# A pruned matmul whose first tiles use packed weights: eight tiles with the upper K half packed in place of seven tiles with both halves

## The chip, the cores and the metric

The kernel runs on one core of one Trainium2 chip. The time is that of the device, in microseconds (us). Most executions agree within 0.3%. All runs compared here are in the fast state, with a granted TensorE clock of 1.0 (0.998 at the least) unless a number says otherwise.

A profile is taken of one execution per kernel. Its span, from the first to the last instruction, is about 2 us shorter than the time. PE is TensorE (matmuls), PEld its weight loads, DVE VectorE, ACT ScalarE, POOL GpSimd, SP the engine that issues most DMAs. HBM is the memory outside the core (DRAM in the kernel's words), SBUF the memory inside it that the engines work from, PSUM the banks that TensorE writes its sums to. K is the dimension that a matmul sums over.

## The reference, cut to what matters

```python
B, S, D = 16, 512, 1024                      # bf16
wg   = w.reshape(256, 4, 1024)               # groups of 4 along K
mag  = abs(wg)
thr  = second largest of each group of 4
wp   = (wg * (mag >= thr)).reshape(1024, 1024)
out  = x @ wp + b                            # x: 8192 rows of 1024
```

In tiles of 128 rows that is 64 row tiles. Each needs 16 matmuls of 512 columns: 8 slices of K times 2 halves of the output columns.

Of the kernel before, what the change touches and what calls it, by code (L numbers as in the profile page):

```python
# [10 lines left out]
def kernel(  # L11
# [28 lines left out]
    NPK = 7  # L40
    batches = []
    t0 = NPK
    while t0 < NT:
        nb = min((5, 4)[len(batches)] if len(batches) < 2 else 8, NT - t0)
        batches.append((t0, nb))
        t0 += nb

    const = ctx.enter_context(tc.tile_pool(name="const", bufs=1))
    dram = ctx.enter_context(tc.tile_pool(name="dram", bufs=1, space=bass.MemoryType.DRAM))
# [7 lines left out]

    def rows(t):
        if t < NPK:
            return of[:NPK * P].rearrange("(p t) f -> p t f", t=NPK)[:, t, :]  # L60
        return of[t * P:(t + 1) * P, :]
# [21 lines left out]

    zeros = const.tile([P, P], bf16)
    dve(nc.vector.memset(zeros[:], 0.0))  # L85
    spark = const.tile([P, P], bf16)

# [4 lines left out]
    xv = xf[:NPK * P].rearrange("(p t) k -> p t k", t=NPK)  # L92
# [9 lines left out]
    def load_x(ta, tb, g, eng="sp"):  # L102
        xs = const.tile([P, tb - ta, HK], bf16, name=f"x_{ta}_{g}")
        issue(eng, xs[:], xv[:, ta:tb, g * HK:(g + 1) * HK])
        for t in range(ta, tb):
            x_sb[(t, g)] = xs[:, t - ta, :]


    load_w(0, 0, 256)
    load_x(6, 7, 0, "act")  # L110
    act(nc.scalar.activation(spark[:, :1], zeros[:, :1], Act.Abs))
    load_x(4, 6, 0)
    load_x(2, 4, 0)
    load_w(0, 256, 512)
    load_x(6, 7, 1)
    load_x(1, 2, 0)
    load_w(1, 256, 512)
    load_x(2, 4, 1)
    load_w(1, 0, 256)
    load_x(4, 6, 1)  # L120
    load_w(0, 512, 1024)
    load_x(0, 2, 1)
    load_x(0, 1, 0)
    load_w(1, 512, 1024)
    sp(nc.sync.dma_start(bias_sb[:], b.partition_broadcast(P)))


    pieces = [(0, 0, 256), (0, 256, 512), (1, 0, 256), (1, 256, 512), (0, 512, 1024), (1, 512, 1024)]
# [12 lines left out]
    scratch = dram.tile([D, Dout], bf16, name="wp_scratch")  # L141
    scr_pk = scratch.rearrange("(g q m) f -> q g m f", g=G, m=4)
    scr_nat = scratch.rearrange("(kt p) f -> p kt f", p=P)
# [40 lines left out]
    def save(g, c0, c1, eng="sp"):  # L184
        issue(eng, scr_pk[:, g, :, c0:c1], wp[:, g, :, c0:c1])

    def reload(h):
        fs = slice(h * FH, (h + 1) * FH)
        sp(nc.sync.dma_start(wp_nat[:, :, fs], scr_nat[:, :, fs]))

    xpk = {}

    def transpose(t, g):


        xg = x_sb[(t, g)].rearrange("p (q m) -> p m q", m=4)
        tp = psum_t.tile([P, 4, P], bf16, name="tp")
        for m in range(4):
            pe(nc.tensor.transpose(tp[:, m, :], xg[:, m, :], ident[:]))  # L199
        xpk[(t, g)] = tp  # L200

    def copy_xt(t, g):
        xt = xtp.tile([P, 4, P], bf16, name=f"xt{g}")
        act(nc.scalar.copy(xt[:].bitcast(fp32), xpk[(t, g)][:].bitcast(fp32)))  # L204
        xpk[(t, g)] = [xt[:, m, :] for m in range(4)]

    ps_open = {}

    part = {"": slice(0, 4), "x": slice(0, 2), "y": slice(2, 4)}
    opened = []  # L210
    left = {}

    def mm_piece(t, i, ms):
        g, c0, c1 = pieces[i]
        h = c0 // FH
        new = (t, h) not in ps_open
        if new:
            ps_open[(t, h)] = psum_o.tile([P, FH], fp32, name="ps")
            opened.append((t, h))
            left[(t, h)] = sum(4 for pc in pieces if pc[1] // FH == h)  # L220
        ps = ps_open[(t, h)]
        for m in range(ms.start, ms.stop):
            left[(t, h)] -= 1
            pe(nc.tensor.matmul(ps[:, c0 - h * FH:c1 - h * FH], lhsT=xpk[(t, g)][m],  # L224
                                rhs=wp[:, g, m, c0:c1],
                                start=(new and m == ms.start), stop=(left[(t, h)] == 0),
                                skip_group_check=True))
# [3 lines left out]
    def stage(t):  # L231
        st = stg.tile([P, FH], fp32, name="st")
        act(nc.scalar.copy(st[:], ps_open.pop((t, 0))[:]))  # L233
        staged[t] = st

    def finish(t):
        o = outp.tile([P, Dout], bf16, name="o")
        dve(nc.vector.tensor_tensor(o[:, FH:], ps_open.pop((t, 1))[:], bias_sb[:, FH:], op=Alu.add))  # L238
        dve(nc.vector.tensor_tensor(o[:, :FH], staged.pop(t)[:], bias_sb[:, :FH], op=Alu.add))  # L239
        issue("act", rows(t), o[:])  # L240

    xnat = {}

    def load_batch(bi):
        if bi >= len(batches):
            return
        tb, nb = batches[bi]
        xb = xtb.tile([P, KT, 8 * P], bf16, name="xb")
        sp(nc.sync.dma_start_transpose(out=xb[:, :, :nb * P], in_=xf[tb * P:(tb + nb) * P, :]))
        for j in range(nb):  # L250
            xnat[tb + j] = xb[:, :, j * P:(j + 1) * P]



# [3 lines left out]
            "T6a F5 T5a T4a F6 T3a T2a F7 M5.0y M4.0y M6.0y M2.0y M5.0x M3.0x T6b T1a M6.0x M3.0y "  # L258
            "M4.0x M2.0x M1.0y M1.0x T3b T2b M6.1 M4.1 M3.1 T4b M1.1 M5.1 T5b M2.1 M6.3 M3.3 M4.3 "
            "T1b T0b M5.3 M2.3 M1.3 M3.2 M6.2 M5.2 T0a M4.2 M2.2 M1.2 M0.0y M0.1 M0.2 M0.3 M0.0x "  # L260
            "M2.4 M3.4 M1.4 M0.4 M5.4 M4.4 M5.5 M2.5 M1.5 M4.5 M6.4 M0.5 M6.5 M3.5"
        ),
        "dve": (
            "abs0 hi0 lo0 t10 t20 thr0 mask0y mask0x mult0y abs1 mult0x hi1 lo1 t11 t21 thr1 mask1 "
            "mult1 lo3 hi3 t23 t13 thr3 mask3 mult3 lo2 hi2 t22 t12 thr2 mask2 mult2 lo4 hi4 t24 "
            "t14 thr4 mask4 mult4 hi5 lo5 t25 t15 thr5 mask5 mult5"
        ),
        "act": (
            "C6a C5a C4a C2a C3a C6b C1a abs3 C3b abs2 C2b C4b C5b abs4 C1b abs5 C0a S5 C0b S1 S4 "
            "S6 S2 S0 S3 W5 W4"  # L270
# [4 lines left out]

    halves = {0: ('x', 'y')}
# [10 lines left out]
    def needs(eng, tok):  # L287
# [7 lines left out]
        if base[0] == "M":  # L295
            t, i = base[1:].split(".")
            key = (int(t), pieces[int(i)][1] // FH)
            slot = []
            if key not in opened and len(opened) >= 6:
                pt, ph = opened[len(opened) - 6]  # L300
                slot = [f"S{pt}"] if ph == 0 else []
            return [f"C{t}{'ab'[pieces[int(i)][0]]}", f"mult{i}{k}"] + slot
        if tok[0] == "S":
            return [f"M{tok[1:]}.{n}" for i, pc in enumerate(pieces) if pc[1] < FH for n in all_of(str(i), i)]
        if tok[0] == "W":
            return all_of("mult" + tok[1:], int(tok[1:]))
# [5 lines left out]
    def emit(eng, tok):  # L312
        base, k = split_tok(tok)
        if tok[0] == "T":
            transpose(int(tok[1]), "ab".index(tok[2]))
# [3 lines left out]
        elif tok[0] == "C":  # L319
            copy_xt(int(tok[1]), "ab".index(tok[2]))  # L320
        elif tok[0] == "M":
            mm_piece(*map(int, base[1:].split(".")), part[k])
        elif tok[0] == "S":
            stage(int(tok[1:]))
        elif tok[0] == "W":
            save(*pieces[int(tok[1:])], eng="act")
        else:
            i = int(base[-1])
            if i not in p:
                p[i] = Piece(i)  # L330
            if eng == "act":
                p[i].abs_act()
            else:
                p[i].do(base[:-1], part[k])
# [14 lines left out]
    save(0, 0, 256)  # L349
    save(0, 256, 512)  # L350
    save(1, 0, 256)
    save(1, 256, 512)
    load_batch(0)
    reload(0)
    reload(1)
    load_batch(1)
    load_batch(2)
    for t in (2, 0, 3, 1, 6, 5, 4):
        finish(t)


    def nat_group(xt, ps, c0, c1):
        for kt in range(KT):
            pe(nc.tensor.matmul(ps, lhsT=xt[:, kt, :], rhs=wp_nat[:, kt, c0:c1],  # L364
                                start=(kt == 0), stop=(kt == KT - 1)))

    def evac(o, ps, c0, c1):
        dve(nc.vector.tensor_tensor(o[:, c0:c1], ps, bias_sb[:, c0:c1], op=Alu.add))  # L368
# [3 lines left out]

    for bi, (tb, nb) in enumerate(batches):
        load_batch(bi + 3)
        if bi == 0:
            outs = [outp.tile([P, Dout], bf16, name="o") for _ in range(nb)]
            for h in range(2):
                for j in range(nb):
                    ps = psum_o.tile([P, FH], fp32, name="ps")
                    nat_group(xnat[tb + j], ps[:], h * FH, (h + 1) * FH)  # L380
                    evac(outs[j], ps[:], h * FH, (h + 1) * FH)
                    if h == 1:
                        store("act", tb + j, outs[j])
            continue
        for j in range(nb):
# [3 lines left out]
            if t == NT - 1:  # L389
                for n, (c0, c1) in enumerate(((0, FH), (FH, FH + CW), (FH + CW, Dout - P), (Dout - P, Dout))):  # L390
                    ps = psum_o.tile([P, FH], fp32, name="ps")
                    nat_group(xt, ps[:, :c1 - c0], c0, c1)
                    evac(o, ps[:, :c1 - c0], c0, c1)
                    store("act" if n % 2 else "sp", t, o, c0, c1)
            else:
                pss = [psum_o.tile([P, FH], fp32, name="ps") for _ in range(2)]
                for kt in range(KT):
                    for h in range(2):
                        pe(nc.tensor.matmul(pss[h][:], lhsT=xt[:, kt, :],  # L399
                                            rhs=wp_nat[:, kt, h * FH:(h + 1) * FH],  # L400
                                            start=(kt == 0), stop=(kt == KT - 1)))
                for h in range(2):
                    evac(o, pss[h][:], h * FH, (h + 1) * FH)
                    if t >= NT - 6:
                        store("act", t, o, h * FH, (h + 1) * FH)
                if t < NT - 6:
# [31 lines left out]
```

## The kernel before: the parts that the change and the argument touch

The pruning compares the four rows of a group. The kernel loads w "packed", with partition q holding rows 4q to 4q+3 side by side, so that the comparison stays inside a partition. A matmul with packed weights needs x permuted in the same way. The first tiles get that from TensorE transposes. All later tiles use "natural" weights (partition = row of K) and take x from transposing DMA loads.

The name `g` is the K half (0 upper, 1 lower) and `h` the half of the output columns. Pruned packed weights reach the natural layout through a scratch tensor in DRAM:

```python
NPK = 7                                           # tiles with packed weights, both K halves
xv = xf[:NPK*P].rearrange("(p t) k -> p t k", t=NPK)     # rows 14 KB apart
pieces = [(0,0,256),(0,256,512),(1,0,256),(1,256,512),(0,512,1024),(1,512,1024)]
... # order lists: T = transpose, C = copy, M tile.piece = products, S = stage PSUM, F = filler
run({eng: order[eng].split() for eng in order})
save(0, 0, 256); save(0, 256, 512); save(1, 0, 256); save(1, 256, 512)   # pruned -> DRAM, SP queue
load_batch(0)                                     # transposing DMA load, 5 tiles
reload(0); reload(1)                              # DRAM -> natural weights, 1 MB each
load_batch(1); load_batch(2)
for t in (2, 0, 3, 1, 6, 5, 4): finish(t)         # bias added, row stored
... # then 57 tiles with natural weights, 16 matmuls each
```

PSUM has six banks for products. The fillers `F` are matmuls on zeros that keep TensorE busy at the start.

## Time and profile before

| | before |
|---|---|
| time, median of 4 runs | 235.28 us (235.03 to 235.44) |
| span of the profiled run | 232.9 us |
| first product with packed weights | 6.86 us |
| first product with natural weights | 33.19 us |
| TensorE idle from the first product to the last | 0.0 us |
| HBM read / written | 6.29 / 18.87 MB |

"Idle" is my own sum over the trace. It takes the starts of consecutive matmuls, and counts what they lie apart beyond 0.216 us (512 columns), 0.109 (256) or 0.056 (128). A distance of exactly two steps is not counted: it is a matmul whose record is missing. The trace of before lacks 20 (1164 matmuls to 1184 weight loads).

These are lines of the profile page of before: busy times, the chain of waits by engine, the costliest groups (line, engine, operation, operands, count, then busy us and mean ns, then idle), and one DMA issue with its us to landing.

```profile
PE 228.2 (98%) x1164; PEld 112.6 (48%) x1184; DVE 104.2 (45%) x177; ACT 15.2 (7%) x27; POOL 0.7 (0%) x6
...
PE 98%; issue 1%; DVE 0%
...
L399 PE MATMUL ps<-wp_nat,xb 128*128 128x512 bf16 x800 | 175.4, 379 | 0.8
...
L199 PE MATMUL tp<-ident,x 128*128 128x128 bf16 x56 | 4.8, 221 | 0.0
...
wp_nat<-wp_scratch SPq DMA_DIRECT2D x2, 1024.0 KB, 6.3
```

TensorE is the limit: 98% of the chain that ended last. A mean of 379 ns for a 512-column matmul is not its cost, because matmuls overlap. The cost is the distance between starts, 0.216 us.

The chain of waits of before, in order of time (start us, length us, what), shows the same without any other engine in it:

```profile
6.89 1.44 PE ps L224 x12
...
21.54 10.74 PE ps L224 x49
...
32.33 1.03 PE ps L224 x4
33.35 9.71 PE ps L364 x45
```

L224 are packed products and L364 the first natural ones. TensorE goes from one to the other at 33.2 us without a gap. Each of the two reloads brings one half of the output columns. The first had landed at 29.5 us. The second landed at 38.9 us; its columns are wanted only after the first half of five tiles, 40 matmuls of 0.216 us later, at about 41.8.

### The profile page before, as it was taken

The numbers are of one execution on the slowest core, as the hardware profiler recorded it, in microseconds if no ns is written. First come the engines' busy times: TensorE is split into PE (matmuls) and PEld (weight loads), VectorE is DVE, ScalarE is ACT, GpSimd is POOL, SyncE is SP. The second block draws the span as 40 slices with busy tenths as digits, with TensorE's granted clock in tenths as the row PEclk, the third lists the DMA queues.
The fourth block names the chain that finished last, engine by engine and source line by source line (L and its number), as shares of the span: only waits on it lengthen the run. The fifth ranks groups of instructions, "written<-read, shape, count | busy, mean of one in ns | idle before, by whom it ended". The sixth has DMA issues, their size and how long they took to land.

```text
span 232.9 us, 2851 instructions
## 1 busy us (share of the span) xinstructions
PE 228.2 (98%) x1164; PEld 112.6 (48%) x1184; DVE 104.2 (45%) x177; ACT 15.2 (7%) x27; POOL 0.7 (0%) x6
## 2 busy tenths in 40 slices
PE   8999999999999999999999999999999999999995
PEld 5997444444444444444444444444444444444443
DVE  3999559533244244244234334334324424423434
ACT  4678000000000000000000000000000000000000
POOL 1000000000000000000000000000000000000000
PEclk9999999999999999999999999999999999999999
DMA  6999969999999952992239821696221221122122
GB/s 191 327 303 242 322 217 223 297 267 256 243 332 261 259 160 77 225 266 98 90 81 274 231 92 45 156 254 178 90 90 54 83 93 64 71 90 91 48 89 90
DMA packets 79500, 40.29 MB, mean 173 GB/s; under 512 B 60416, under 2 KB 71936, under 8 KB 79488
## 3 DMA queue, kind: packets, MB, share of 16 engines
q1 hardware_dynamic: 68208, 22.32, 43.3%
q10 hardware_dynamic: 11280, 17.80, 23.1%
q8 instruction: 9, 0.15, 0.3%
q14 instruction: 3, 0.02, 0.0%
HBM read 6.29 MB, written 18.87 MB: 108 GB/s over the span
## 4 chain that ended last, share of the span: by engine, by line
PE 98%; issue 1%; DVE 0%
PE ps L399 75%; PE ps L224 10%; PE ps L364 9%; PE ps L136 2%; PE tp L199 1%; DVE o L368 0%; DVE zeros L85 0%
## 5 line engine op out<-in xcount | busy, mean ns | idle before, releaser
L399 PE MATMUL ps<-wp_nat,xb 128*128 128x512 bf16 x800 | 175.4, 379 | 0.8
L368 DVE TENSOR_TENSOR o<-ps,bias_sb 128x512 bf16<-128x512 f32 (+1 forms) x116 | 74.0, 677 | 117.2 <-PE ps L399 106.5
L399 PEld LDWEIGHTS <-xb 128*128 128x128 bf16 x816 | 79.8, 98 | 96.4
L224 PE MATMUL ps<-wp,xt 128*128 128x256 bf16 (+1 forms) x166 | 25.3, 307 | 0.1
L364 PE MATMUL ps<-wp_nat,xb 128*128 128x512 bf16 (+2 forms) x110 | 21.0, 348 | 0.1
L224 PEld LDWEIGHTS <-xt 128*128 128x128 bf16 x168 | 16.2, 98 | 7.6
L364 PEld LDWEIGHTS <-xb 128*128 128x128 bf16 x112 | 10.4, 98 | 10.7
L238 DVE TENSOR_TENSOR o<-ps,bias_sb 128x512 bf16<-128x512 f32 x7 | 4.8, 686 | 4.9 <-PE ps L224 4.9
L136 PE MATMUL ps<-zeros 128*128 128x128 bf16 (+1 forms) x32 | 5.1, 320 | 1.0 <-DVE zeros L85 1.0
L159 ACT ACTIVATE mag<-w_sb 128x1024 bf16<-128x1024 bf16 (+1 forms) x4 | 6.0, 1489 | 0.8 <-DMA w_sb<-in_w_dram 0.8
L156 DVE TENSOR_TENSOR wp<-w_sb,mag 128x1024 bf16<-128x1024 bf16 (+2 forms) x7 | 5.4, 765 | 0.2
L156 DVE TENSOR_TENSOR mag<-mag,hi 128x1024 bf16<-128x1024 bf16 (+2 forms) x7 | 5.3, 767 | 0.2
L204 ACT COPY xt<-tp 128x256 f32<-128x256 f32 x14 | 5.0, 372 | 5.2 <-PE tp L199 5.1
L199 PE MATMUL tp<-ident,x 128*128 128x128 bf16 x56 | 4.8, 221 | 0.0
L239 DVE TENSOR_TENSOR o<-st,bias_sb 128x512 bf16<-128x512 f32 x7 | 4.8, 681 | 0.0
L199 PEld LDWEIGHTS <-x 128*128 128x128 bf16 x56 | 4.1, 115 | 0.1
L136 PEld LDWEIGHTS <-zeros 128*128 128x128 bf16 x32 | 2.8, 118 | 2.6 <-issue 1.7
L233 ACT COPY st<-ps 128x512 f32<-128x512 f32 x7 | 3.6, 609 | 0.1
L156 DVE TENSOR_TENSOR hi<-mag 128x512 bf16<-128x512 bf16 (+1 forms) x6 | 3.0, 508 | 0.0
L156 DVE TENSOR_TENSOR lo<-mag 128x512 bf16<-128x512 bf16 (+1 forms) x6 | 3.0, 506 | 0.0
L156 DVE TENSOR_TENSOR hi<-hi,lo 128x256 bf16<-128x256 bf16 (+1 forms) x6 | 2.0, 336 | 0.2
L166 DVE TENSOR_SCALAR mag<-w_sb 128x1024 uint16<-128x1024 uint16 x2 | 0.8, 424 | 2.8 <-DMA w_sb<-in_w_dram 2.8
(11 smaller groups left out, 6.4 us busy)
## 6 DMA issues: line engine op xcount, KB each, us to landing
out_dram<-o ACTq DMA_DIRECT2D x58, 256.0 KB, 3.9
wp_nat<-wp_scratch SPq DMA_DIRECT2D x2, 1024.0 KB, 6.3
x<-in_x_dram SPq DMA_DIRECT2D x5, 256.0 KB, 4.7
out_dram<-o ACTq DMA_DIRECT2D x10, 128.0 KB, 1.7
w_sb<-in_w_dram SPq DMA_DIRECT2D x4, 256.0 KB, 4.2
w_sb<-in_w_dram SPq DMA_DIRECT2D x2, 512.0 KB, 7.0
wp_scratch<-wp SPq DMA_DIRECT2D x4, 256.0 KB, 5.7
wp_scratch<-wp ACTq DMA_DIRECT2D x2, 512.0 KB, 5.3
```

The source lines that it names most:

```text
L136: pe(nc.tensor.matmul(warm_ps[:, :rep * P], lhsT=zeros[:], rhs=zeros[:, None, :].to_broadcast([P, rep, P]), start=True, stop=True))
L156: dve(nc.vector.tensor_tensor(out, a, b_, op=op))
L159: act(nc.scalar.activation(self.mag[:], self.w, Act.Abs))
L199: pe(nc.tensor.transpose(tp[:, m, :], xg[:, m, :], ident[:]))
L204: act(nc.scalar.copy(xt[:].bitcast(fp32), xpk[(t, g)][:].bitcast(fp32)))
L224: pe(nc.tensor.matmul(ps[:, c0 - h * FH:c1 - h * FH], lhsT=xpk[(t, g)][m], rhs=wp[:, g, m, c0:c1], start=(new and m == ms.start), stop=(le ...
L233: act(nc.scalar.copy(st[:], ps_open.pop((t, 0))[:]))
L238: dve(nc.vector.tensor_tensor(o[:, FH:], ps_open.pop((t, 1))[:], bias_sb[:, FH:], op=Alu.add))
L239: dve(nc.vector.tensor_tensor(o[:, :FH], staged.pop(t)[:], bias_sb[:, :FH], op=Alu.add))
L364: pe(nc.tensor.matmul(ps, lhsT=xt[:, kt, :], rhs=wp_nat[:, kt, c0:c1], start=(kt == 0), stop=(kt == KT - 1)))
L368: dve(nc.vector.tensor_tensor(o[:, c0:c1], ps, bias_sb[:, c0:c1], op=Alu.add))
L399: pe(nc.tensor.matmul(pss[h][:], lhsT=xt[:, kt, :], rhs=wp_nat[:, kt, h * FH:(h + 1) * FH], start=(kt == 0), stop=(kt == KT - 1)))
```

## The change

The intent is to give TensorE less to do and to drop the trip through DRAM. Eight early tiles take packed weights for the upper K half only. Their partial sums are staged in SBUF. POOL adds the bias to them there, and the lower K half is done later with natural weights and added by VectorE when PSUM is emptied. Natural weights are made by "spreading": 16 SBUF-to-SBUF DMAs of 128 KB each, four for each K half and column half. Three natural tiles are opened (upper K half, six PSUM banks) while the lower weights are still on their way. The 22 "closings" of four matmuls each follow.

```diff
-    NPK = 7
+    NPK = 8
+    LEAD = 3
+    GT = 4
-    xv = xf[:NPK * P].rearrange("(p t) k -> p t k", t=NPK)
+    xv = xf[:NPK * P].rearrange("(u p t) k -> p u t k", p=P, t=GT)
@@ front loads: x upper half only, bias no longer here @@
-    load_x(6, 7, 1)
...
-    sp(nc.sync.dma_start(bias_sb[:], b.partition_broadcast(P)))
-    pieces = [(0, 0, 256), (0, 256, 512), (1, 0, 256), (1, 256, 512), (0, 512, 1024), (1, 512, 1024)]
+    pieces = [(0, 0, 256), (0, 256, 512), (0, 512, 768), (0, 768, 1024), (1, 0, 512), (1, 512, 1024)]
@@
+    def spread(g, c0, c1, eng="sp"):
+        for k in range(4):
+            issue(eng, wp_nat[:, 4 * g + k, c0:c1], wp[32 * k:32 * k + 32, g, :, c0:c1])
@@ after the packed products @@
-    save(0, 0, 256)
... (saves, reloads)
+    xlow = xtb.tile([P, KT, 8 * P], bf16, name="xb")
+    def load_low(u):
+        cols = slice(u * GT * P, (u + 1) * GT * P)
+        sp(nc.sync.dma_start_transpose(out=xlow[:, 4:, cols], in_=xf[cols, HK:]))
+        ...
+    spread(0, 0, FH)
+    xnat.update(load_nat(NPK, NPK + LEAD))
+    spread(0, FH, Dout)
+    xnat.update(load_low(0))
+    spread(1, 0, FH)
+    xnat.update(load_low(1))
+    spread(1, FH, Dout)
+    load_batch(0)
+    act(nc.scalar.dma_start(bias_sb[:], b.partition_broadcast(P)))
... (POOL: 16 additions of the bias to staged sums)
+    for j, h in [(0, 0), (1, 0), (2, 0), (0, 1), (1, 1), (2, 1)]:
+        open_nat(j, h)
+    for t, h in closes:
+        close(t, h)
```

The order lists of PE, DVE and ACT were rewritten to match, the batches are cut differently, and the last nine tiles (before: six) store in two halves.

## The prediction

> **What bounds the kernel now.** TensorE, from start to end: the chain of waits is 98% PE, the granted clock 1.00. The first product with packed weights starts at 6.89 us, the last PE work ends at about 230.3, and the sum of PE work explains all of the 223.4 us between:
> - 896 weight loads and matmuls of 512 columns on natural weights. 816 of them took 50.50 to 226.74 us, 0.216 us each: 193.5 us. (The Trainium skill, "TensorE: Matmul & The Clock Gate", section "Wait - 56ns, not 53.3ns?", gives 215.7 ns; the trace agrees.)
> - 112 packed products of 256 columns at 0.109 and 56 of 512 columns: 24.3 us.
> - 36 transposes after 6.89 us at 0.056 us: 2.0 us.
> - the last tile in pieces: 3.5 us.
>
> Sum 223.3. So before has no stall to win back: after 6.89 us PE always has something to do. The DRAM round trip of the pruned weights is hidden behind packed products.
>
> **What the change does.**
> - PE: packed products fall to 8 tiles x 16 of 256 columns, 14.0 us; transposes after the first product fall from 36 to 12, 0.67 us; natural matmuls become 944 x 0.216 = 203.9 us; last tile 3.5. Sum 222.1: 1.3 us less. Nearly all of it is transposes, wholly on the critical path.
> - Removed: 2 MB written to and 2 MB read from DRAM; 0.75 MB of early x loads. Added: 16 SBUF-to-SBUF DMAs of 128 KB (about 0.6 us of SP issue each), two transposing loads of half rows, 9 more PSUM stagings on ACT (0.61 us each), 16 bias additions on POOL. All off the critical path unless late.
> - First packed product: same chain, still about 6.9 us.
>
> **Deadlines (estimates from before's durations).** Packed work ends at 6.9 + 14.0 + 0.7 + 0.1 = about 21.7 us.
> - Upper natural weights, first half: pruned at 10.4, issued by 12.8, landed by about 17; wanted 21.7. The transposing load of three tiles: 1.2 us issue per tile, landing 3.5 later, about 20; wanted 21.7.
> - Lower half, columns 0-511: pruned at about 21.3, issued by 23.7, landed 26 to 27; wanted at 26.9, after 24 matmuls. The tightest: stall 0 to 1 us.
> - Lower half, columns 512-1023: pruned 26.4, landed about 31.5; wanted 33.
> - Bias, now issued only after the last staging, at about 23, landing 27 to 29: PSUM's six banks run out at 29.6.
> - POOL: about 1.1 us per addition (estimate; Trainium skill, "GPSIMD Engine Reference", section "Elementwise - side-by-side cycle accounting", 2.6 cycles per element; before has no such instruction). Sixteen take 18 us from about 28; PE's closings run from 27 to 46 us. POOL may lag 1 to 2 us, within the banks' slack.
> - The first batch of 8 reuses the buffer of the lower-half x, free at 46; lands 60 to 62, wanted 63.3.
>
> With 0.4 us of stalls in sum: 235.34 - 1.3 + 0.4 = **234.4 us**, range 233.2 to 236.4. Faster by over 2% (below 230.6) needs more PE work gone than there is: 0.02. Slower by over 2% needs 6 us of stalls: 0.04. Within 2%: 0.94.
>
> **What would show it.** Right: packed products end near 21.7, no more than 12 transposes after the first, the chain of waits stays over 97% PE; first packed product to PE's end 222 to 223 us. Wrong: PE gaps at about 22, 27, 30 or 63 us released by DMA into the natural weights, by VectorE (bias or POOL late) or by the transposing load; or a matmul with strided x weights over 0.216 us.
>
> **What would make it wrong.** Slow spreading DMAs; POOL at 2 us per addition or slowing VectorE; the bias late.

## The result, and the profile after

| | before | after |
|---|---|---|
| time, median of 4 runs | 235.28 us | 236.01 us (235.82 to 236.25) |
| ratio, 95% interval | | 1.0033 (1.0015 to 1.005) |
| span of the profiled run | 232.9 us | 234.3 us |
| first packed product | 6.86 us | 7.49 us |
| first natural product | 33.19 us | 22.13 us |
| idle of TensorE after the first product | 0.0 us | 2.14 us |
| HBM read / written | 6.29 / 18.87 MB | 3.41 / 16.78 MB |

Ratios are the mean time of one kernel's fast runs over that of the other's of the same rounds, so not quite the ratio of the medians quoted. The change is 0.3% slower. That is "the same" by a 2% rule, but the interval lies above 1. I had forecast 0.9 us less, and it was 0.7 us more.

The same lines of the page, after:

```profile
PE 228.5 (98%) x1167; PEld 112.9 (48%) x1167; DVE 105.1 (45%) x179; ACT 17.7 (8%) x30; POOL 18.8 (8%) x23
...
PE 88%; DVE 4%; DMA 4%; ACT 2%; SPq 0%; issue 0%
...
L343 PE MATMUL ps<-wp_nat,xb 128*128 128x512 bf16 (+1 forms) x976 | 208.0, 375 | 1.5 <-DMA wp_nat<-wp 1.4
...
L339 POOL TENSOR_TENSOR st<-st,bias_sb 128x512 f32<-128x512 f32 x16 | 17.9, 1155 | 0.2 <-DMA bias_sb<-in_b_dram 0.2
...
L183 PE MATMUL tp<-ident,x 128*128 128x128 bf16 x32 | 2.8, 219 | 0.3 <-DMA x<-in_x_dram 0.3
...
wp_nat<-wp SPq DMA_DIRECT2D x16, 128.0 KB, 3.2
```

Transposes fell from 56 to 32, as meant. The share of PE in the chain fell from 98 to 88%, and a DMA into the natural weights stands in it. The busy share of PE (98% in both) hides this: matmuls overlap, and the few that waited have modelled ends.

The chain of waits of after, in order of time, where it leaves TensorE:

```profile
15.00 1.81 ACT mag L152
...
20.68 1.22 DVE wp L149
...
23.25 0.60 SPq L97
...
23.90 5.82 DMA wp_nat<-wp
...
29.76 201.92 PE ps L343 x950
```

This is the hand-over to the lower K half. ACT takes absolute values, VectorE prunes (done at 21.9 us), SP issues the third set of copies, and one of them, issued at 23.9, lands 5.8 us later. After that it is TensorE to the end.

Weight loads of TensorE in that stretch (start us, busy us, engine, line, operation, and in brackets the idle time before). The profile puts the waits down to "issue", but the starts follow the landings of the four copies (27.5, 28.0, 29.7 and 30.1 us):

```profile
22.02 5.17 PEld L343 LDWEIGHTS <-xb 128*128 128x128 bf16 x25
27.57 0.10 PEld L343 LDWEIGHTS <-xb 128*128 128x128 bf16 x1 [0.38 <-issue]
28.04 0.10 PEld L343 LDWEIGHTS <-xb 128*128 128x128 bf16 x1 [0.38 <-issue]
29.77 0.10 PEld L343 LDWEIGHTS <-xb 128*128 128x128 bf16 x1 [1.63 <-issue]
30.10 4.00 PEld L343 LDWEIGHTS <-xb 128*128 128x128 bf16 x19 [0.24 <-issue]
```

The 24 opening matmuls end at 27.3 us, and the fourth closing matmul starts at 30.1. That is the idle time of 2.14 us.

The other loss is at the front. The first step of VectorE waits for the first weights. In before it starts at 3.73 us:

```profile
3.73 0.43 DVE L166 TENSOR_SCALAR mag<-w_sb 128x1024 uint16<-128x1024 uint16 x1 [2.79 <-DMA w_sb<-in_w_dram]
```

In after it starts at 4.36 us, although the load is the same instruction, issued at the same 0.73 us:

```profile
4.36 0.43 DVE L159 TENSOR_SCALAR mag<-w_sb 128x1024 uint16<-128x1024 uint16 x1 [3.42 <-DMA w_sb<-in_w_dram]
```

The account closes. Working time from the first product to the last matmul's start is 230.01 - 6.86 = 223.15 us before and 231.46 - 7.49 - 2.14 = 221.83 us after: 1.32 us less. Add 0.63 us for the later first product and 2.14 us of idle: -1.32 + 0.63 + 2.14 = 1.45, and the spans differ by 1.4 us.

So the gain is there. The question is why the two waits arose.

### The profile page after: what moved, and what is told of

The parts are those of the page before. It is cut to its first block, busy times and chain, and to the rows that moved or that the text cites. A ratio compares the mean times of both kernels' runs of the same rounds, so it can differ in the third digit from the quotient of the medians.

```text
span 234.3 us, 2884 instructions
## 1 busy us (share of the span) xinstructions
PE 228.5 (98%) x1167; PEld 112.9 (48%) x1167; DVE 105.1 (45%) x179; ACT 17.7 (8%) x30; POOL 18.8 (8%) x23
## 3 DMA queue, kind: packets, MB, share of 16 engines
HBM read 3.41 MB, written 16.78 MB: 86 GB/s over the span
## 4 chain that ended last, share of the span: by engine, by line
PE 88%; DVE 4%; DMA 4%; ACT 2%; SPq 0%; issue 0%
PE ps L343 86%; DMA wp_nat<-wp 2%; PE ps L205 2%; DMA w_sb<-in_w_dram 2%; DVE hi L149 1%; DVE lo L149 1%; ACT st L214 1%; DVE mag L149 1%; ACT mag L152 1%; DVE wp L149 1%; SPq L97 0%; PE tp L183 0%; DVE mag L159 0%; DVE o L347 0%
## 5 line engine op out<-in xcount | busy, mean ns | idle before, releaser
L343 PE MATMUL ps<-wp_nat,xb 128*128 128x512 bf16 (+1 forms) x976 | 208.0, 375 | 1.5 <-DMA wp_nat<-wp 1.4
L343 PEld LDWEIGHTS <-xb 128*128 128x128 bf16 x976 | 95.8, 99 | 113.6 <-issue 2.6
L339 POOL TENSOR_TENSOR st<-st,bias_sb 128x512 f32<-128x512 f32 x16 | 17.9, 1155 | 0.2 <-DMA bias_sb<-in_b_dram 0.2
L205 PE MATMUL ps<-wp,xt 128*128 128x256 bf16 x128 | 14.5, 272 | 0.3 <-DVE wp L149 0.3
L205 PEld LDWEIGHTS <-xt 128*128 128x128 bf16 x128 | 12.4, 98 | 1.8 <-issue 0.4
L347 DVE TENSOR_TENSOR o<-ps,st 128x512 bf16<-128x512 f32 x16 | 11.0, 691 | 3.1 <-PE ps L343 2.2
L214 ACT COPY st<-ps 128x512 f32<-128x512 f32 x16 | 8.3, 648 | 0.3 <-PE ps L205 0.3
L149 DVE TENSOR_TENSOR wp<-w_sb,mag 128x512 bf16<-128x512 bf16 (+2 forms) x8 | 5.4, 688 | 0.1
L149 DVE TENSOR_TENSOR mag<-mag,hi 128x512 bf16<-128x512 bf16 (+2 forms) x8 | 5.3, 688 | 0.1
L188 ACT COPY xt<-tp 128x256 f32<-128x256 f32 x8 | 2.7, 371 | 4.7 <-PE tp L183 4.7
L335 POOL COPY pruned<-wp 128x1 bf16<-128x1 bf16 x1 | 0.2, 186 | 25.5 <-DVE wp L149 25.5
```

Of the source, the lines that this page charges most:

```text
L149: dve(nc.vector.tensor_tensor(out, a, b_, op=op))
L188: act(nc.scalar.copy(xt[:].bitcast(fp32), xpk[t][:].bitcast(fp32)))
L205: pe(nc.tensor.matmul(ps[:, c0 - h * FH:c1 - h * FH], lhsT=xpk[t][:, m, :], rhs=wp[:, g, m, c0:c1], start=(new and m == ms.start), stop=(l ...
L214: act(nc.scalar.copy(st[:], ps_open.pop((t, h))[:]))
L335: pool(nc.gpsimd.tensor_copy(out=pruned[:], in_=wp[:, 1, 3, Dout - 1:]))
L339: pool(nc.gpsimd.tensor_tensor(staged[(t, h)][:], staged[(t, h)][:], bias_sb[:, h * FH:(h + 1) * FH], op=Alu.add))
```

## The experiments

The suspects for the late third set of copies were:

- **Q**, the queue. The Trainium skill, "DMA: Bandwidth & Descriptors", section "Queues, rings and completion order", says that each DMA engine takes descriptors in ring order. The third set stands in the SP queue behind the transposing load of the lower x.
- **B**, the bias. Its broadcast now runs from 22.3 to 27.1 us. The same page, section "Issuing engines are not separate DMA queues", says that the ACT and SP queues share the 16 DMA engines.
- **S**, one slow engine: if a copy is spread over several DMA engines and has landed only when the last of them is done, one engine that lags holds it up.
- **P**, late pruning: VectorE waited 0.77 us for ACT.

For the front there was **X**, the step between the rows that the early x loads read.

What the trace of after says before any experiment: DMA of 22.7 to 24.2 us, when three of the four copies had been issued.

```profile
DMA packets 1509, 0.42 MB, mean 281 GB/s; under 512 B 1485, under 2 KB 1485, under 8 KB 1509
## 3 DMA queue, kind: packets, MB, share of 16 engines
q1 hardware_dynamic: 1485, 0.37, 110.1%
```

No packet of 1 KB, the size of these copies, is among them. All on the SP queue (q1) are the small packets of the transposing load before them; the first 1 KB packet starts at 24.7, 2.0 us after the first issue. That speaks for Q, but only in this trace: in c0, e1, e2 and e5, which have the same order, it starts 1.2 to 1.3 us after the issue, and in e3, with no transposing load ahead, 1.2 us after it. And DMA of 27.8 to 29.5 us in 40 slices:

```profile
DMA  9190009000000001001001010010100100000000
...
DMA packets 47, 0.02 MB, mean 13 GB/s; under 512 B 33, under 2 KB 47, under 8 KB 47
```

Nearly nothing moves. The packet records show about one 1 KB packet at a time, of 0.1 us each, while 21 of the 256 B packets of the next transposing load, begun between 27.5 and 28.1 us, all end at 29.94 to 29.98, up to 2.5 us later. At 27.5 us, too, begins a packet of 16 KB on the queue that the page calls "instruction" (0.97 us). I read this as S: one engine is behind and the others wait for it. The trace does not name the engine of a packet, so it stays a reading.

### c0_control: the changed kernel again

No edit.

> The changed kernel once more, unaltered. If the two losses of its first trace belong to the kernel: 1.002 to 1.005 of before, first packed product again at 7.3 to 7.6 us, TensorE idle about 2 us between 27 and 30 us for the lower half's first natural weights, whose last copy lands 5 to 6 us after its issue. If they were accidents of one execution: first product at 6.9 us or no idle at 27 us in this trace, and a ratio of 0.995 to 1.000.

Measured: 235.78 us against 235.20, ratio 1.0036 (1.0018 to 1.0054). First product 7.62 us, idle 1.41 us, all of it at the hand-over. The third set was issued at 22.1, 22.7, 23.3 and 24.0 us and landed at 25.0, 27.3, 27.7 and 29.5. Both losses belong to the kernel. The size of the idle time varies.

### e1_bias_early: the bias with the front loads

```diff
     load_w(1, 512, 1024)
+    sp(nc.sync.dma_start(bias_sb[:], b.partition_broadcast(P)))
-    act(nc.scalar.dma_start(bias_sb[:], b.partition_broadcast(P)))
```

> The bias is loaded at the end of the front loads, as before did, so its 256 KB leave the window 22 to 27 us. Theory B (the bias broadcast shares the DMA engines with the third set of spreading copies and makes them late): their issue-to-landing falls from about 5.5 us to 3 to 4, TensorE's idle time near 27 us from about 2.1 us to under 0.7, time 1.5 us less. Theory Q (the copies stand in the SP queue's rings behind the transposing load of the lower x, issued just before them): landing stays at 4.5 us or more, idle falls by under 0.7 us. Theory S (one DMA engine is held by a fetch of TensorE instructions): landing stays over 4.5 us and a 16 KB packet still lies inside the stretch.

Measured: 235.23 us, ratio 0.9998 (0.9985 to 1.0011), so 0.4% faster than the control on the same chip. Idle at the hand-over 0.58 us. Two of the four copies now landed 2.8 and 3.0 us after their issue (2.9 and 4.6 in the control). The other two, issued at 23.9 and 24.5, still landed at 28.8 and 29.0, with the 16 KB packet at 26.7. B is part of it and not all. The gain of 0.9 us is less than the 1.5 that I expected of B alone. The shorter idle time flatters the edit: the last copy landed only 0.5 us earlier than in the control, and TensorE began its natural products 0.36 us later (22.64 against 22.28), having waited 0.56 us for early x at 10.8.

### e2_abs4_early: ACT's fifth absolute value three stagings earlier

```diff
-  S4h0 S5h0 S2h0 S7h0 S3h0 abs4
+  S4h0 S5h0 abs4 S2h0 S7h0 S3h0
```

> ACT takes the absolute value of the fifth piece three stagings earlier. Theory P (the pruning of that piece is late because VectorE waited 0.77 us for ACT): its last product is done 0.6 to 0.8 us earlier (about 21.2 us in place of 21.9), the copies are issued that much earlier if the SP queue is free (it is free at 22.6 only), so under theory Q the idle time at 27 us falls by under 0.3 us and the time is the same within 0.4 us; if the pruning alone sets it, the idle time and the time fall by 0.7 us.

Measured: 235.85 us, ratio 1.0039 (1.0024 to 1.0054), the same as the control. In the profiled run the early loads were late (ACT waited 1.06 us for weights, TensorE 0.85 us for x) and the pruning ended at 21.7 us, only 0.2 us sooner. So as a test of P this run is inconclusive; moving the step gained no time. It showed something else. TensorE lost 1.7 us earlier (first natural product at 23.84 us), came to the lower weights at 29.0, and did not wait there: all copies had landed by 28.3. The time was as before. An earlier delay of TensorE had merely taken the place of the wait.

### e3_low_later: the copies ahead of the lower-x loads

```diff
     spread(0, FH, Dout)
-    xnat.update(load_low(0))
     spread(1, 0, FH)
-    xnat.update(load_low(1))
+    xnat.update(load_low(0))
     spread(1, FH, Dout)
+    xnat.update(load_low(1))
```

> The third set of spreading copies goes ahead of the transposing load of the lower x of tiles 0 to 3 (which follows it), and the fourth set ahead of that of tiles 4 to 7. Theory Q: the copies' first data packets start within 1 us of the issue, issue-to-landing falls from 5.5 to 3 to 4 us, TensorE's idle time at 27 us shrinks by 1.5 us or more; the lower x now lands near 30 us, when its first use is due, so a new wait of up to 1 us may appear there. Theory B or S: landing stays at 4.5 us or more and the idle time stays near 2 us.

Measured: 242.62 us, ratio 1.0316 (1.0287 to 1.0345). A miss, and a lesson. The wait moved to the lower x, as the waits of this run show (who waited for whom: us in total, times, longest):

```profile
PE ps L343 <- DMA xb<-in_x_dram: 4.8, 1, 4.8
...
PE ps L343 <- DMA wp_nat<-wp: 0.2, 1, 0.2
```

The first lower-x load landed at 30.6 us, but TensorE went on at 36.0, when the second had landed. Both loads write one tile, interleaved by K slice, and in the built program the second matmul of the first lower-x closing waits for the second DMA, which brings nothing that it reads. This false wait is in the changed kernel too, where the second load (landing at 31.9 us, wanted at 32.3) came just in time. More was lost after it: from 36 to 41 us the trace shows a granted clock of 0.50 and matmuls 0.43 us apart, which is 2.5 us in sum. (The granted clock over the whole run was 0.986 to 0.993 in this kernel's executions.)

### e6_low_split: the same order, two tiles for the lower x

```diff
-    xlow = xtb.tile([P, KT, 8 * P], bf16, name="xb")
+    xlow = [const.tile([P, 4, GT * P], bf16, name=f"xlow{u}") for u in range(2)]
```

and the order of e3_low_later.

> The order of e3_low_later, but the lower x of tiles 0 to 3 and of 4 to 7 stand in two tiles, so that the first use waits for its own load alone. If the 5 us that e3 lost were that false wait: it is gone, ratio to before 0.997 to 1.003, and the reading of theory Q is clean: issue-to-landing of the third set of copies 3 to 4.4 us, TensorE idle under 1 us near 28 us, and under 1 us more for the lower x near 31 us. If it was the late transposing load itself: still 2 us or more of waiting for x near 31 us.

Measured: 235.17 us against 235.07, ratio 0.9999 (0.9972 to 1.0026). The 5 us are gone (and the slow matmuls after them), so they were the false wait. Idle at the hand-over was 0.57 us. The first of the third set landed 2.8 us after its issue, but the last two (24.0 and 24.7) landed at 29.0 and 29.4, with the 16 KB packet at 26.7. The time gained against the changed kernel is about 0.35%, the same size as for B, but from other rounds on another chip, and the two intervals just overlap. The trace does not show how it was gained: the last copy landed at 29.4 us against 29.5 in the control, and the idle time is shorter because TensorE, after early waits of 0.6 us, came to the natural products 0.7 us later (23.00). Only the second copy was clearly sooner, 3.6 us after its issue against 4.6. So Q is at most a part. The run carries the split tile too. In the changed kernel the false wait cost nothing (31.9 us against 32.3), so I put the gain down to the order; the split alone was not run.

### e5_x_rows and b2_before_x_rows: the step between the early rows

In the changed kernel, the early tiles take consecutive rows (2 KB apart) in place of every fourth (8 KB); the outputs likewise:

```diff
-    xv = xf[:NPK * P].rearrange("(u p t) k -> p u t k", p=P, t=GT)
+    xv = xf[:NPK * P].rearrange("(u t p) k -> p u t k", p=P, t=GT)
```

> One thing changed: the eight early tiles take consecutive rows (partition p of tile t is row 128t+p, 2 KB apart) in place of every fourth row (8 KB apart; before has 14 KB). Theory X (the early loads are slow because of the 8 KB step between the rows that they read): the first weights land at 3.7 us as in before, not 4.35, the first packed product starts at 6.9 and not 7.5 us, TensorE has no wait for early x, and the time falls by 0.5 to 1 us at most (part may be given back at the wait near 27 us, which then starts earlier). Rival (the step does not matter; the front is late because of which loads stand in it): first weights again at 4.3 us, same time.

In the kernel before, the same in place of every seventh row (14 KB):

```diff
-    xv = xf[:NPK * P].rearrange("(p t) k -> p t k", t=NPK)
+    xv = xf[:NPK * P].rearrange("(t p) k -> p t k", t=NPK)
```

> The kernel before with its seven early tiles on consecutive rows (2 KB apart) in place of every seventh row (14 KB apart); nothing else. Theory X in its wider form (14 KB is a good step for these loads, and both 8 KB and 2 KB are worse): the early loads bring 2.2 MB and not 2.4 in the first 10 us, the first packed product or later ones wait, ratio to before 1.002 to 1.006. Rival (the step does not matter, the changed kernel's front is late for what stands in it): 2.4 MB in 10 us, same time within 0.1%.

Kernel before, unaltered, for a second trace:

> The kernel before, unaltered, for a second trace: so far its front is known from one execution. If that one was typical: first weights land at 3.0 us after issue (first VectorE step at 3.7), first packed product at 6.8 to 7.0 us, TensorE without any idle time of 0.1 us to its end. If it was a lucky one: first weights at 4.3 us as in the changed kernel, first product at 7.4 or later.

Measured: e5_x_rows 236.24 us against 235.07, ratio 1.0042 (1.0017 to 1.0066), no gain. b2_before_x_rows 1.0002 (0.9962 to 1.0043), no difference within that interval; its first product came at 7.51 us, and its trace has a wait of 1.5 us for a transposing load at 52.6. b1_before_again, a single run: 234.99 us, first product 7.16 us, idle 0.0. With it and c0_control the account closes a second time: -1.31 + 0.46 + 1.41 = 0.56, and the spans differ by 0.55 us. All traces, sorted by row step:

| step | traces | first x tile, us to landing | first weights, us to landing |
|---|---|---|---|
| 14 KB | 2 | 2.1, 2.2 | 3.0, 3.0 |
| 2 KB | 4 | 2.1, 2.1, 2.3, 2.3 | 3.1, 3.2, 3.1, 3.1 |
| 8 KB | 8 | 2.4 to 2.7 | 3.5 to 3.8 |

X is right for the first weights. They always follow the first x tile, issued beside them on the ACT queue, and only with the 8 KB step do they land 0.5 us late. X is not enough for what matters, the first product, which came no earlier in e5_x_rows (7.76 us). There it did not wait for VectorE. In before and after the first product follows VectorE's first step by 3.13 us; in e5 that step began at 3.97, so VectorE was ready at about 7.1. TensorE was still at its own early transposes and fillers, as its matmuls in after and then in e5 show:

```profile
5.34 0.72 PE L128 MATMUL ps<-zeros 128*128 128x128 bf16 x10
...
7.49 1.25 PE L205 MATMUL ps<-wp,xt 128*128 128x256 bf16 x10 [0.30 <-DVE wp L149]
```

```profile
5.53 1.27 PE L128 MATMUL ps<-zeros 128*128 128x128 bf16 x10
...
7.54 0.38 PE L183 MATMUL tp<-ident,x 128*128 128x128 bf16 x4
7.76 1.25 PE L205 MATMUL ps<-wp,xt 128*128 128x256 bf16 x10
```

From the first of the ten fillers to the next group TensorE took 0.62 us in after and 1.07 in e5; why is not shown. The later front loads came late as well: by 10 us, 2.18 MB had come in e5_x_rows, 2.39 MB in after and 2.43 in before. But the step alone does not explain that, since e3_low_later with the 8 KB step had 2.17 MB and b2_before_x_rows with 2 KB had 2.34. No run joins the 2 KB step with fewer fillers.

### e7 and e8: removals together

e7_combo_low_first has consecutive rows, the early bias, the split tile, and this order: `spread(0,0)`, three natural tiles, `load_low(0)`, the other three spreads, `load_low(1)`. e8_combo_low_later has the order of e3_low_later in its place.

> All removals at once: consecutive rows, bias with the front loads, two tiles for the lower x, and the first lower-x load ahead of the second set of copies, so that the third set has only copies before it in the queue. If X, B and Q each hold: first packed product 6.9 us, all copies landed by their first use, TensorE idle under 0.5 us, span near 231.5, ratio 0.993 to 0.996 (the 1.3 us of transposes that the change removed, and no loss). If instead the prune chain of VectorE sets the end whatever the DMAs do: idle of 1 us or more at the third or fourth set, ratio 0.998 or more.

> As e7, but with the lower-x loads each behind the copies of the lower weights. Expected if X, B and Q hold: copies on time, but the first lower x lands near 30 us where TensorE wants it at 29 to 29.5; idle 0.5 to 1 us, ratio 0.995 to 0.998, so a little behind e7.

Measured: e7 235.19 us, 0.9999 (0.9973 to 1.0025); e8 235.21 us, 0.9994 (0.9966 to 1.0022). Both fell short. The hand-over was nearly clean (idle there 0.15 us in e7, none in e8), but TensorE had already waited 0.8 and 1.2 us for early x and weights. So the 2 KB rows, which these two carry along, brought nothing here; whether they caused these waits is not shown.

### e9_all: the removals with the kernel's own rows and a mended front

e6_low_split with the early bias, and:

```diff
-    load_w(0, 512, 1024)
+    load_w(0, 512, 768)
     load_x(0, 2)
+    load_w(0, 768, 1024)
-            "T7a F2 T5a F10 T4a T3a F5 T2a ...
+            "T7a F2 T5a F3 T4a T3a F1 T2a ...
```

> The changed kernel with its own rows, the bias in front, two tiles for the lower x, the copies ahead of the lower-x loads, the load of the third and fourth pieces of weights split in two with the early x between, and 11 fillers fewer in the front. Expected: idle time of TensorE after the first product 0.3 to 0.8 us in place of 2.1, first product at 7.4 (VectorE sets it, the fillers do not), span 232.3 to 233.0, ratio 0.995 to 0.998. If the front gives nothing and only the hand-over matters: 0.999 to 1.000 as e1 and e6.

Measured: 234.73 us against 235.29 of before, ratio 0.996 (0.9926 to 0.9995), one run in the slow state left out (the fast runs of before range from 234.97 to 237.18 us in these rounds). Idle after the first product: 0.0 us. The chain of waits of e9, by engine, and its TensorE matmuls over the hand-over:

```profile
PE 96%; DMA 2%; DVE 1%; issue 0%
```

```profile
19.75 2.67 PE L207 MATMUL ps<-wp,xt 128*128 128x256 bf16 x23
22.26 7.93 PE L344 MATMUL ps<-wp_nat,xb 128*128 128x512 bf16 x36
30.03 3.62 PE L344 MATMUL ps<-wp_nat,xlow 128*128 128x512 bf16 x16
```

No bracket, so no idle time: three groups follow each other. From first product to last matmul's start it is 229.44 - 7.62 = 221.82 us, which is the working time of the changed kernel (221.83) to a hundredth. The third set was issued at 22.1 to 23.9 us and landed at 24.6, 25.6, 26.0 and 26.8; wanted at 27.4. What is left of the loss is the first product at 7.62 us. How much of the clean hand-over is owed to which of the edits was not tested; the cut of the fillers bears on it too, as the end of the next table shows.

### e10_first_x_later: the first x tile after the table load

```diff
-    load_x(7, 8, "act")
     act(nc.scalar.activation(spark[:], zeros[:, :1], Act.Abs))
+    load_x(7, 8, "act")
```

on top of e9_all.

> e9_all with one more edit: the load of the first x tile is issued on the ACT queue after the activation-table load (at about 2.7 us), not before it (0.7 us), so that the first weights have the DMA engines to themselves. If that x load, with its 8 KB step, is what makes the first weights land 0.6 us later than in the kernel before: they land 3.0 us after their issue, VectorE starts at 3.75 and not 4.4 us, first product at 6.9 to 7.1 us, span 231.7 to 232.0, ratio 0.993 to 0.995, TensorE still without idle after it. If the first weights are late for another reason: VectorE at 4.3 or later, ratio as e9 (0.996) or worse.

Measured: 234.69 us against 235.35, ratio 0.9969 (0.9955 to 0.9983). The edit did not do what I meant. The x load was issued at 0.97 us in place of 0.73, not at 2.7: ACT's queue issued it while the table load was running. The first weights landed 3.8 us after their issue, again behind the x tile. So it says nothing against the reading that the x tile holds them back, and does not prove it. TensorE also waited 0.2 us for x at 64.1 us. The run confirms that the mended kernel beats before by 0.3%.

### What the third set of copies tells in all traces

| run | issued, first to last | landed, first to last | 16 KB packet at | idle at hand-over |
|---|---|---|---|---|
| after | 22.7 to 24.5 | 27.5 to 30.1 | 27.5 | 2.14 |
| c0_control | 22.1 to 24.0 | 25.0 to 29.5 | 27.3 | 1.41 |
| e1 (no bias there) | 22.7 to 24.5 | 25.5 to 29.0 | 26.7 | 0.58 |
| e6 (no x load ahead) | 22.8 to 24.7 | 25.6 to 29.4 | 26.7 | 0.57 |
| e8 (neither) | 23.1 to 25.0 | 25.6 to 29.0 | 26.4 | 0.00 |
| e2 | 22.5 to 24.3 | 25.2 to 28.3 | 28.9 | 0.00 |
| e9 (neither) | 22.1 to 23.9 | 24.6 to 26.8 | 28.5 | 0.00 |

In all eight traces where a copy was still in flight when the 16 KB packet began (the first five rows, e3, e5 and e7), the last copy landed 2.2 to 2.6 us after that packet's start. Where the set had landed before it, there was no such tail. In e9 the packet fell into the fourth set, whose first copy then took 4.1 us and not 2.7; TensorE did not need it yet. The first set agrees: in all eleven traces a 16 KB packet began between 11.8 and 13.5 us, and the first copy landed 2.2 to 2.6 us after it. That is strong agreement for S. But it is not an experiment on S alone: no run moved the packet and nothing else.

Q and B do not decide the outcome by themselves. e2 has both, and its copies were out of the way before the packet came; e8 has neither, and its last copy was caught. What differs is the packet's moment, and that goes with TensorE's own progress: in all fourteen traces it began when TensorE had started 207 to 218 weight loads of the program, and the later ones about every 128 (110 to 142). A filler has a weight load too. With 11 fillers fewer in e9 and e10, the packet came 6.0 to 6.3 us after the first natural product; in the nine other variants it was 3.2 to 5.4. So the cut of the fillers is a rival to Q and B in explaining the clean hand-over of e9, and no run separates them.

## Why the prediction was right or wrong

- **"Sum 222.1: 1.3 us less."** Right to a few hundredths. Measured without idle time: 223.15 us in both traces of before, 221.83 and 221.82 in after and e9. The step of 0.216 us for a 512-column matmul, which the Trainium skill, "TensorE: Matmul & The Clock Gate", section "Wait — 56ns, not 53.3ns?", gives as 215.7 ns, held in both kernels, also with strided x as weights (their weight loads took at most 115 ns).
- **"With 0.4 us of stalls in sum."** This term failed. It was 2.14 us in the first trace and 1.41 in the second. I had named the place ("Lower half, columns 0-511 ... The tightest: stall 0 to 1 us") but mis-sized it. Pruned at about 21.3: it was 21.9. Issued by 23.7: the last issue began at 24.5 and ended at 25.2. Landed 26 to 27: it was 30.1. The landing I took from copies on a quiet queue. In its place the runs show copies that took 4.7 to 5.8 us from issue to landing in after and 2.9 to 5.5 in c0_control: beside the bias (shown by e1 in part), behind a transposing load (seen in the first trace, at most a part by e6), and with the last of them in flight when the 16 KB packet came (agreement in eight of eight traces, no experiment). The prediction's own signs of being wrong came in: TensorE gaps at 27 to 30 us released by DMA into the natural weights, and 88% of PE in the chain in place of over 97%.
- **"First packed product: same chain, still about 6.9 us."** Wrong by 0.6 us: 7.49, and 7.40 to 7.88 in every variant. The chain of instructions was the same, and VectorE took 3.13 us from its first step to the first product in both first traces. The landing of the first weights was not the same (3.6 us against 3.0), and the x load beside them had another row step. Setting that right in e5 did not bring the product forward, because TensorE's own front then came later; and before itself had 7.16 in its second trace. I had priced the front loads by their bytes.
- **The bias "landing 27 to 29".** Right (27.1), and harmless where I looked, at the PSUM banks. Its harm was to the copies beside it.
- **POOL "about 1.1 us per addition".** Right: 1.156 us. The estimate is from the Trainium skill, "GPSIMD Engine Reference", section "3.1 Elementwise — side-by-side cycle accounting". VectorE waited 0.9 us in sum for POOL, inside the slack of the banks.
- **"Slow spreading DMAs"**, which I feared, came in the third set only: the fourth, with a free queue, landed 2.7 to 3.4 us after its issue.
- **The total.** 236.01 us lies in the range, and "within 2%" was right. The sign was wrong: 0.9 us faster was forecast, 0.7 us slower came. That it still lay in the range is owed to the width of the range, not to the terms.

## What to carry to other kernels

When TensorE never idles, removing work from it pays exactly that work, but only if every hand-over stays on time; a change that shortens the packed stage by 11 us also moves each later deadline 11 us forward. Price a DMA on a deadline by what runs beside it and by the longest landing that a trace shows for its like, not by its bytes alone: here 2.7 us in one set was 5.8 in another. Put loads that nobody waits for behind the copies that somebody waits for, give tiles with separate readers separate buffers, and sum busy time and idle time apart: the busy share of TensorE was 98% in the good and the bad version alike.

## What the Trainium skill lacked or had wrong

- No page tells what a 16 KB packet of the instruction queue does to copies in flight. "Runtime: NRT & Kernel Launch", section "Instruction fetch mechanics", calls the cost of crossing a 16 KiB block of instructions "mostly hidden". Here such a packet took 0.88 to 1.34 us in the stretch that matters, and copies in flight landed 2.2 to 2.6 us after its start in eight of eight traces.
- "DMA: Bandwidth & Descriptors", section "DMA Transpose (X-bar)", does not say how long packets of a transposing load can take. Here 256 B packets that took 0.018 us at the median took up to 2.49 us, and the DMA engines moved 13 GB/s for 1.7 us.
- The same page lists row pitches from 512 KiB up in "Latency and other measured facts". A step of 8 KB between 1 KB reads already cost 0.2 to 0.6 us against 14 KB on a 128 KB load, and 0.5 to 0.8 us on the weights issued beside it.
- No page has timings of copies between partitions of SBUF that the SP queue issues: 128 KB in 1 KB runs took 0.6 us to issue and, in the fourth set of after with a free queue, 2.7 to 3.4 us to land.
- "GPSIMD Engine Reference" was right: 2.6 cycles per element at 1.2 GHz give 1.109 us for 512 elements (an estimate from that page), measured 1.156.
